# An RWKV-6 block with a two-level expert gate: pairs of heads in a fixed, two-deep engine order, the gate in one pass, whole rows scattered into 224 places per expert

## The chip, the cores and the metric

One Trainium2 chip, one NeuronCore. The metric is the device time of one execution in microseconds (us); three runs of the kernel before gave 718.98, 717.66 and 714.95, median 717.66. Engines are PE (TensorE; PEld is its weight load), DVE (VectorE), ACT (ScalarE), POOL (GpSimd) and SP (SyncE, which issues most DMAs).

## The reference

An RWKV-6 recurrence over 4 batches, 8 heads, 768 steps, head size 48, then a mixture of 16 experts (4 groups of 4) over the 3,072 tokens with 384 channels:

```python
for t in range(S):
    cur = einsum('bhd,bhe->bhde', u * k[t], v[t])
    y[t] = einsum('bhd,bhde->bhe', r[t], state + cur)
    state = w[t][..., None] * state + einsum('bhd,bhe->bhde', k[t], v[t])
x = y as (B*S, H*D)
g = argmax(x @ w_group);  e = argmax(x @ w_expert[g])
out = softmax_g * softmax_e * (relu(x @ w1[g, e]) @ w2[g, e])
```

All of it is float32.

## The kernel before

**First stage, pairs.** Two heads of one batch form a pair; 16 pairs are worked off, each over 6 chunks of 128 steps (12 blocks of 64). `decays` (L240 to L272) runs on DVE and ACT: a reversed scan of the decays (`s`, L248), its reciprocals (L253, L255), a forward scan (`e`, L257), the scaled keys `kk` (L261) and queries `q` (L265), and on ACT `ru` and `tb` (L269, L270). `pair` (L274 to L364) is then a chain through PE: scores of `kk` and `q` and of `k` and `ru` (L282), masked on DVE into `at` (L289, L292); `kk` transposed into `kt` (L299, L301); `kt` times values, the growth of the states (L310), copied by ACT into `g` (L316); a scan on DVE over blocks, `zs` (L320); the inner part, values times `at` (L330); the cross part, `zs` times `q`, into the same banks (L347; half of it waits for a small POOL instruction, `mark`, L338, that follows the inner part); a copy to `xt` (L354), six transposes (L360) and a copy into the token rows `x` (L362). `decays(n+1)` is written ahead of `pair(n)`. All PE results of this stage share one pool of four tiles of two PSUM banks, `banks`.

**Gate.** After four pairs `logits` (L366 on) writes the batch's rows to `x_scratch` in DRAM and makes 24 products with `wr` (20 columns each, L375). `gate` (L381 to L429) runs once a batch, one batch late: it chooses a group, then an expert in it (`choose` twice, L133 to L152), gets each token's rank in its expert by two products with a triangle and with ones (L387, L388) and a loop of 12 small DVE instructions over the chunks, turns the rank into a place, and scatters (token, weight), 8 bytes a token, in six indirect DMAs on POOL's queue (L427). Each of them waits for the one before it, since all write `slot_scratch`.

**Second stage, experts.** Each of 16 experts has 256 static places, two tiles of 128; unused places hold a token number out of bounds. One DMA reads all places (`slots`, L493); two indirect DMAs on POOL fetch an expert's rows from `x_scratch` (L498, 128 rows of 1,536 bytes each); `expert` (L512) transposes them (L519, copy L521), makes the hidden layer in 24 products with 256 columns (L508, relu on ACT L510), the output in 16 products with 384 columns (L527), scales it (L531) and scatters it to `out` (L533). Weights of two experts are held. Beside the first four experts `look` (L538 on) reduces the decays twice a batch (L543, L544) to see whether a slow path is needed. Tokens beyond 256 go through a loop at the end, which runs zero times here.

**What sets the order.** Engines run in order. The program is written pair by pair, but a scheduler that estimates durations reorders each engine's instructions, so that DVE's list mixes pairs, gate and `look`; SP's and POOL's lists are made the same way.

Of the kernel before, what the change touches and what calls it, by code (L numbers as in the profile page):

```python
# [34 lines left out]
C = 64  # L36
JT = 2
CAP = JT * 128
# [5 lines left out]
def rwkv_then_moe(  # L44
# [24 lines left out]
    OV = N - CAP  # L69
    OVT = OV // 128  # L70
    NSTAT = NE * CAP
    NSLOT = NSTAT + NE * OV
    halves = [slice(0, 64), slice(64, 128)]

    x_dram = nc.dram_tensor("x_scratch", (N + 1, DM), F32, kind="Internal").ap()
    slot_dram = nc.dram_tensor("slot_scratch", (NSLOT, 2), F32, kind="Internal").ap()
# [32 lines left out]
    eidx = numbers([128, NE], [[1, NE]], 0, "eidx")  # L109
    thresh = numbers([128, OVT], [[128, OVT]], CAP, "thresh")  # L110
# [8 lines left out]

    seen = const([128, NE], F32, "seen")  # L120
    nc.vector.memset(seen, 0.0)
# [10 lines left out]
    def choose(pool, z, k, n):  # L132


        def small(name, shape):
            return pool.tile([128, n] + shape, F32, name=name, tag=name)

        top, sums = small(f"top{k}", []), small(f"sum{k}", [])
        low, one = small(f"low{k}", [4]), small(f"one{k}", [4])
        nc.vector.tensor_reduce(out=top, in_=z, axis=AX.X, op=ALU.max)  # L140
        tb = top[:, :, None].to_broadcast([128, n, 4])
# [3 lines left out]
        nc.vector.tensor_reduce(out=sums, in_=low, axis=AX.X, op=ALU.add)  # L145
        nc.vector.tensor_scalar(out=sums, in0=sums, scalar1=1e-9, scalar2=None, op0=ALU.add)
        db = desc[:, None, :].to_broadcast([128, n, 4])
        nc.vector.tensor_tensor(out=one, in0=one, in1=db, op=ALU.mult)
        best = small(f"best{k}", [])
        nc.vector.tensor_reduce(out=best, in_=one, axis=AX.X, op=ALU.max)  # L150
        nc.vector.tensor_tensor(out=one, in0=db, op=ALU.is_equal,
                                in1=best[:, :, None].to_broadcast([128, n, 4]))  # L152
        return sums, one

    def experts_of(pool, lg, n, weight):

        gsum, gone = choose(pool, lg[:, :, 0:G], 0, n)
        el = pool.tile([128, n, Eg], F32, name="el", tag="el")
        el4 = pool.tile([128, n, G, Eg], F32, name="el4", tag="el4")
        gob = gone[:, :, :, None].to_broadcast([128, n, G, Eg])  # L160
        nc.vector.tensor_tensor(
            out=el4, in0=lg[:, :, G:].rearrange("p c (g e) -> p c g e", g=G), in1=gob,
            op=ALU.mult)
# [11 lines left out]
    with ExitStack() as first:  # L175
# [6 lines left out]
        def banks():  # L182
            return pp.tile([128, 1024], F32, name="banks", tag="banks")
# [90 lines left out]
        def pair(p, v, xt, x):  # L274
# [28 lines left out]
            def value(c, t, m):  # L303
                o = (c * H + 2 * hp + t) * D
                return v[:, o:o + m]
# [426 lines left out]
```

## Time and profile before

| | us |
|---|---|
| median of 3 runs | 717.66 |
| the profiled execution: its time / its span | 719.73 / 718.0 |
| busy: PE, PEld, DVE, ACT, POOL | 549.1, 439.0, 237.4, 131.8, 106.9 |
| mean granted PE clock | 0.845 of 2.4 GHz |
| from span start to the first score product | 22.3 |
| pairs and gates, to the last logits | 22.3 to 290.9 |
| last gate and hand-over to the experts | 290.9 to 338.4 |
| 16 experts | 338.4 to 702.6 |
| end (last scatter, counters, end of program) | 702.6 to 718.0 |

The shares of busy time are an average over stages with different limits, so each stage is read by itself: in a view of stretches for the busy time of each engine and PE's granted clock (1.00 is 2.4 GHz, 0.50 is 1.2 GHz), and in the timeline for what ended each wait.

### The profile page before, as it was taken

To read this page: it belongs to the slowest core of one execution; us is meant where nothing else is said; L and a number is where in the kernel's file an instruction comes from. 1 tells how busy PE (TensorE), PEld (TensorE's weight loads), DVE (VectorE), ACT (ScalarE), POOL (GpSimd) and SP (SyncE) were. 2 spreads that over 40 slices of the span, in tenths; PEclk is the share of its full clock that TensorE was granted. 3 is DMA by queue.
4 is the path that set the end of the run, shared out by engine and by line. 5 is a ranking of instruction groups with operands and counts; after the bars stand their busy time and mean duration, and the time that the engine had idled before them with its cause. 6 is when DMAs were issued, how large, how long until landed. Compare 5 with 4: busy or idle time off the path is not lost. (4 is left out here: it accounts for less than half of the span.)

```text
span 718.0 us, 12586 instructions
## 1 busy us (share of the span) xinstructions
PE 549.1 (76%) x5490; PEld 439.0 (61%) x5490; DVE 237.4 (33%) x449; ACT 131.8 (18%) x249; POOL 106.9 (15%) x133
## 2 busy tenths in 40 slices
PE   0476886687768688201999999999999999999991
PEld 0466775586658677200776677766777667776670
DVE  3977476638864441664311100111001110011100
ACT  0343233304331321000110111100111001110110
POOL 8000000300030021014022201221112211121100
PEclk9986668756776765555899999999999999999996
DMA  9726358126313004234335445354454635445000
GB/s 218 153 61 164 100 189 275 46 76 155 81 35 100 3 2 134 49 85 113 110 130 214 152 162 192 139 214 138 173 178 153 213 124 191 162 164 193 11 9 20
DMA packets 19777, 91.19 MB, mean 127 GB/s; under 512 B 4585, under 2 KB 7706, under 8 KB 15106
## 3 DMA queue, kind: packets, MB, share of 16 engines
q1 hardware_dynamic: 14850, 79.26, 35.9%
q0 software_dynamic: 4864, 11.04, 4.2%
q8 instruction: 45, 0.74, 0.4%
q14 instruction: 18, 0.15, 0.1%
HBM read 80.43 MB, written 11.43 MB: 128 GB/s over the span
## 5 line engine op out<-in xcount | busy, mean ns | idle before, releaser
L508 PE MATMUL bank_a<-xt,w 128*128 128x256 f32 x768 | 172.3, 385 | 15.4 <-DVE xt L521 15.4
L508 PEld LDWEIGHTS bank_a<-xt,w 128*128 128x128 f32 x768 | 146.2, 192 | 39.0 <-DVE xt L521 19.3
L527 PE MATMUL bank_b<-w,ht 128*128 128x384 f32 x512 | 167.7, 486 | 0.0
L527 PEld LDWEIGHTS bank_b<-w,ht 128*128 128x128 f32 x512 | 97.3, 190 | 64.4
L531 DVE TENSOR_SCALAR yo<-bank_b,slots 128x384 f32<-128x384 f32 x32 | 19.8, 618 | 322.1 <-PE bank_b L527 322.1
L510 ACT ACTIVATE ht<-bank_a 128x256 f32<-128x256 f32 x128 | 49.2, 384 | 349.8 <-PE bank_a L508 349.8
L533 POOL DMA_INDIRECT out_dram<-yo,slots x32 | 32.4, 1014 | 251.6 <-DVE yo L531 243.5
L347 PE MATMUL banks<-q,zs 64*48 64x64 f32 x704 | 41.9, 296 | 36.2 <-DVE zs L320 27.9
L347 PEld LDWEIGHTS banks<-q,zs 64*48 64x48 f32 x704 | 38.3, 198 | 38.9 <-DVE zs L320 30.1
L427 POOL DMA_INDIRECT slot_scratch<-pack,dest x24 | 27.1, 1130 | 110.7 <-DVE dest L425 70.9
L282 PE MATMUL banks<-q,kk 64*64 64x64 f32 x768 | 25.0, 316 | 22.3 <-DVE q L265 22.3
L519 PE MATMUL bank_b<-ident,xg 128*128 128x128 f32 x96 | 13.8, 282 | 36.2 <-DMA xg<-x_scratch,slots 36.2
L375 PEld LDWEIGHTS banks<-wr,xt 128*128 128x128 f32 x192 | 41.5, 333 | 0.0
L375 PE MATMUL banks<-wr,xt 128*128 128x20 f32 x192 | 41.1, 378 | 0.0
L498 POOL DMA_INDIRECT xg<-x_scratch,slots x32 | 30.9, 966 | 61.3 <-PE bank_b L519 52.1
L282 PEld LDWEIGHTS banks<-q,kk 64*64 64x64 f32 x768 | 22.0, 220 | 25.9 <-DVE q L265 22.3
L519 PEld LDWEIGHTS bank_b<-ident,xg 128*128 128x128 f32 x96 | 11.9, 146 | 41.2 <-issue 39.2
L360 PE MATMUL banks<-ident,xt 128*128 128x128 f32 x96 | 24.7, 429 | 14.5 <-ACT xt L354 14.5
L248 DVE TENSOR_TENSOR_SCAN s<-w,first_of 128x780 f32<-128x780 f32 x16 | 28.4, 1773 | 14.8 <-DMA w<-in_w_dram 11.0
L360 PEld LDWEIGHTS banks<-ident,xt 128*128 128x128 f32 x96 | 18.3, 221 | 17.8 <-ACT xt L354 17.8
L257 DVE TENSOR_TENSOR_SCAN e<-w,iv 128x780 f32<-128x780 f32 x16 | 28.5, 1781 | 0.5
L310 PE MATMUL banks<-v,kt 64*64 64x48 f32 x704 | 15.7, 232 | 16.6 <-ACT kt L301 16.6
(120 smaller groups left out, 413.6 us busy)
## 6 DMA issues: line engine op xcount, KB each, us to landing
w<-in_w_dram SPq DMA_DIRECT2D x32, 1536.0 KB, 6.7
rk<-in_rk_dram SPq DMA_DIRECT2D x32, 288.0 KB, 5.0
w<-in_w_dram SPq DMA_DIRECT2D x32, 146.2 KB, 6.2
wt<-in_w_dram SPq DMA_DIRECT2D x4, 1170.0 KB, 7.5
v<-in_v_dram SPq DMA_DIRECT2D x4, 1152.0 KB, 7.4
x_scratch<-x SPq DMA_DIRECT2D x4, 1152.0 KB, 4.8
xg<-x_scratch,slots POOLq DMA_INDIRECT x32, 5.1
out_dram<-yo,slots POOLq DMA_INDIRECT x32, 3.5
```

What stands on the lines that cost most here:

```text
L248: nc.vector.tensor_tensor_scan(out=s[:, 0:WP][:, ::-1], data0=w[:, ::-1], data1=first_of[:, ::-1], initial=1.0, op0=ALU.mult, op1=ALU.add)
L257: nc.vector.tensor_tensor_scan(out=e, data0=w, data1=iv, initial=0.0, op0=ALU.mult, op1=ALU.add)
L282: nc.tensor.matmul(z[halves[j], 512 * t + C * c:512 * t + C * (c + 1)], lhsT=lhs[hs, sl], rhs=rhs[hs, sl], start=True, stop=True)
L347: m = nc.tensor.matmul(y[j][64 * t:64 * t + D, C * c:C * (c + 1)], lhsT=zs[halves[t], :, i], rhs=q[halves[t], C * i:C * (i + 1)], start=Fa ...
L360: nc.tensor.transpose(z[:, c * 128:(c + 1) * 128], xt[:, c * 128:(c + 1) * 128], ident)
L375: nc.tensor.matmul(lv[:, c], lhsT=xts[hp][:, c * 128:(c + 1) * 128], rhs=wr[:, hp], start=(hp == 0), stop=(hp == HP - 1))
L427: nc.gpsimd.indirect_dma_start(out=slot_dram, out_offset=bass.IndirectOffsetOnAxis(ap=dest[:, c:c + 1], axis=0), in_=pack[:, c, :], in_off ...
L498: nc.gpsimd.indirect_dma_start(out=xg, out_offset=None, in_=x_dram, in_offset=bass.IndirectOffsetOnAxis(ap=slot[:, 0:1].bitcast(I32), axis=0))
L508: nc.tensor.matmul(z[:, 0:128 * nt], lhsT=w1[:, dc, f * 128:(f + 1) * 128], rhs=xt[:, dc], start=(dc == 0), stop=(dc == DC - 1))
L510: nc.scalar.activation(out=ht[:, f], in_=z[:, 0:128 * nt], func=AF.Relu)
L527: nc.tensor.matmul(z[:, 0:DM], lhsT=ht[:, f, j * 128:(j + 1) * 128], rhs=w2[:, f], start=(f == 0), stop=(f == FC - 1))
L533: nc.gpsimd.indirect_dma_start(out=out, out_offset=bass.IndirectOffsetOnAxis(ap=slot[:, 0:1].bitcast(I32), axis=0), in_=yo, in_offset=None ...
```

## The change

- **Order.** The pair is cut into pieces, and a loop of 17 rounds writes them out with a fixed order for PE, DVE and ACT. Round n holds the pieces of pair n up to the inner part, the cross part, rows and logits of pair n-1, and the decays of pair n+1. PSUM is split: two score tiles (two banks each), one tile `y` (two banks), two single banks for all else.
- **Logits** are made in two goes: 18 products when three pairs of a batch are done, six after the fourth.
- **Gate.** `choose` runs once on all five groups of four logits (the group's and four experts'); ranks come from a scan over chunks, so the two PE products have 16 columns and the loop over chunks goes.
- **Rows.** `x` is 386 wide (row, token number, weight) and is scattered whole (1,544 bytes a token) into `slot_scratch`, six indirect DMAs with no waits between them; `x_scratch` isn't written on the main path. An expert has 224 places (tiles of 128 and 96), read by two plain DMAs on SP's queue; no gather is left on POOL. Unused places must be filled first: `blanks` writes 16 times 224 rows (346 KB each), four a round in rounds 0 to 3.
- **Experts.** Hidden products have 224 columns.

```diff
-JT = 2
-CAP = JT * 128
+TILES = (128, 96)
+CAP = sum(TILES)
...
-        pp = first.enter_context(tc.tile_pool(name="psum_t", bufs=4, space=PSUM))
+        p_sc = first.enter_context(tc.tile_pool(name="psum_s", bufs=2, space=PSUM))
+        p_y = first.enter_context(tc.tile_pool(name="psum_y", bufs=1, space=PSUM))
+        p_t = first.enter_context(tc.tile_pool(name="psum_t", bufs=2, space=PSUM))
...
+        def blanks(e):
+            nc.sync.dma_start(
+                out=slot_dram[e * NR:e * NR + CAP, :].rearrange("(p j) w -> p (j w)", j=2),
+                in_=blank.rearrange("p j w -> p (j w)"))
...
+        def gate(b, lg, x):
+            mine, gone, low, sums = choose(gp, lg, NCH)
...
+            nc.vector.tensor_tensor_scan(
+                out=upto.rearrange("p e c -> p (e c)"),
+                data0=within.rearrange("p e c -> p (e c)"),
+                data1=mine.rearrange("p e c -> p (e c)"), initial=0.0, op0=ALU.mult, op1=ALU.add)
+            nc.tensor.matmul(cps[:, 0:NE], lhsT=ut, rhs=upto[:, :, NCH - 1], start=True, stop=True)
+            nc.tensor.matmul(cps[:, NE:2 * NE], lhsT=ones, rhs=upto[:, :, NCH - 1], start=True,
+                             stop=True)
...
             for c in range(NCH):
-                nc.gpsimd.indirect_dma_start(
+                put = nc.gpsimd.indirect_dma_start(
                     out=slot_dram,
                     out_offset=bass.IndirectOffsetOnAxis(ap=dest[:, c:c + 1], axis=0),
-                    in_=pack[:, c, :], in_offset=None)
+                    in_=x[:, c, :], in_offset=None)
+                tc.declare_no_dep(put.ins, group="rows", reason="no two tokens have one slot")
...
+        with tc.manual_schedule(engines={ENG.PE, ENG.DVE, ENG.Activation}):
+            for n in range(TOTAL + 1):
+                if n < TOTAL:
+                    p = pipe[n]
...
+                    if n + 1 < TOTAL:
+                        z = pipe[n + 1] = suffixes(n + 1)
+                    masked(p)
+                    if z:
+                        products(z)
+                    keys(p)
+                if n:
+                    outer(pipe[n - 1])
+                if n < TOTAL:
+                    growth(p)
+                    if z:
+                        scaled(z)
+                        prefixes(z)
+                    states(p)
+                    if z:
+                        queries(z)
+                    inner(p)
...
+                    for e in range(4 * n, min(4 * n + 4, NE)):
+                        blanks(e)
...
+                if n:
+                    finish(n - 1)
+                    if ready and (n % HP == 2 or n == TOTAL):
+                        gate(*ready.pop(0))
...
+        for m in TILES:
+            xg = row_tile()
+            nc.sync.dma_start(out=xg[0:m], in_=slot_dram[at:at + m, :])
...
-                nc.tensor.matmul(z[:, 0:128 * nt], lhsT=w1[:, dc, f * 128:(f + 1) * 128],
+                nc.tensor.matmul(z[:, 0:n], lhsT=w1[:, dc, f * 128:(f + 1) * 128],
```

(`suffixes` is the scan `s`, `masked` the scores and the mask, `products` is `kk`, `keys` is `kt`, `outer` the cross part and the copy to `xt`, `growth` and `states` the way to `zs`, `scaled` is `ru` and `tb`, `prefixes` the reciprocals and `e`, `queries` is `q`, `finish` the rows and logits.)

PE, one pair in the middle of a batch. Before (L282 scores, L299 and L360 transposes, L310 growth, L330 inner, L347 cross part):

```order
L282 MATMUL banks<-q,kk 64x64 x24
L282 MATMUL banks<-ru,rk_122 64x64 x24
L299 MATMUL banks<-ident,kk 128x128 x6
L310 MATMUL banks<-v_139,kt 64x48 x22
L330 MATMUL banks<-at,v_139 64x64 x24
L347 MATMUL banks<-q,zs 48x64 x22
L360 MATMUL banks<-ident,xt 128x128 x6
```

One round of the change (L304 scores, L322 transposes, L374 cross part, L335 growth, L355 inner; L398 are the logits at a batch's end):

```order
L304 MATMUL scores<-q,kk 64x64 x24
L304 MATMUL scores<-ru,rk_138 64x64 x24
L322 MATMUL bank<-ident,kk 128x128 x6
L374 MATMUL y<-q,zs 48x64 x22
L335 MATMUL bank<-v_156,kt 64x48 x22
L355 MATMUL y<-at,v_156 64x64 x24
L322 MATMUL bank<-ident,xt 128x128 x6
L398 MATMUL bank<-wr,xt 128x20 x18
```

The seven pieces are the same; the cross part and the second transposes now belong to the pair before and stand where PE had waited for `kt`, `zs` and `xt` of its own pair.

DVE, one round of the change (L258 is `s` and L266, L280, L282, L284, L289 the rest of the next pair's decays; L311, L314 the mask; L345 `zs`):

```order
L258 SCALAR_TENSOR_TENSOR s_178<-w_143,first_of 128x780
L311 TENSOR_TENSOR at<-scores,later 128x768
L314 COPY_PREDICATED at<-diag_mask,scores 128x768
L266 TENSOR_TENSOR kk<-rk_140,s_178 128x768
L280 TENSOR_SCALAR iv_180<-s_178 128x12
L282 RECIPROCAL iv_180<-iv_180 128x12
L284 SCALAR_TENSOR_TENSOR e<-w_143,iv_180 128x780
L345 SCALAR_TENSOR_TENSOR zs<-g_185,tb_183 128x576
L289 TENSOR_TENSOR q<-rk_140,e 128x768
```

Nine instructions a pair as before, now always in this order; the next round's scores wait for the last of them, `q`.

DVE in the last gate of the change, from its first selection to the ranks (L604, L605 are the two reductions of `look`; L408 the scan over chunks):

```order
L159 TENSOR_TENSOR ones_3168<-ones_3168,desc 128x120
L604 TENSOR_REDUCE ends<-wt 96x1
L160 TENSOR_REDUCE best<-ones_3168 128x30
L605 TENSOR_REDUCE ends<-wt 96x1
L161 TENSOR_TENSOR ones_3168<-desc,best 128x120
L166 TENSOR_TENSOR mine<-ones_3168 128x6x16
L408 SCALAR_TENSOR_TENSOR upto_c<-within,mine 128x96
```

Two of `look`'s reductions still stand inside the last gate, ahead of its ranks; before, three of them stood ahead of the places.

## Rows read from the trace of the kernel before

**Rows 1.** Groups of the page: busy, mean ns; idle before, what ended it

```profile
L282 PE MATMUL banks<-q,kk 64*64 64x64 f32 x768 | 25.0, 316 | 22.3 <-DVE q L265 22.3
```

**Rows 2.** Stretches: length, busy by engine (instructions), PE clock, DMA share, GB/s

```profile
core 0: us, PE busy (x) PEld busy (x) DVE busy (x) ACT busy (x) POOL busy (x), PEclk, DMA share, GB/s
280.40:290.90 10.50, 10.47 (x50) 10.35 (x49) 0.00 (x0) 0.64 (x1) 0.00 (x0) 0.50 0.47 148
290.90:338.40 47.50, 1.14 (x4) 0.93 (x4) 29.79 (x64) 0.45 (x2) 9.57 (x10) 0.50 0.38 91
338.40:702.60 364.20, 348.76 (x1378) 255.79 (x1378) 41.05 (x68) 49.17 (x128) 58.53 (x59) 0.99 0.42 150
```

**Rows 3.** Timeline of one pair: start, duration, engine, line, idle before and releaser

```profile
40.00 1.56 PE L282 MATMUL banks<-q,kk 64*64 64x64 f32 x48
41.33 1.50 PE L282 MATMUL banks<-ru,rk 64*64 64x64 f32 x48
...
42.70 0.23 DVE L255 RECIPROCAL iv<-iv 128x12 f32<-128x12 f32 x1
42.77 1.54 PE L299 MATMUL banks<-ident,kk 128*128 128x128 f32 x6
...
42.93 1.01 DVE L292 COPY_PREDICATED at<-diag_mask,banks 128x768 f32<-128x768 uint8 x1
43.84 1.76 DVE L257 TENSOR_TENSOR_SCAN e<-w,iv 128x780 f32<-128x780 f32 x1
...
45.20 0.84 PE L310 MATMUL banks<-v,kt 64*64 64x48 f32 x42 [0.89 <-ACT kt L301]
...
45.93 0.88 PE L330 MATMUL banks<-at,v 64*64 64x64 f32 x46
...
46.91 1.36 DVE L320 TENSOR_TENSOR_SCAN zs<-g,tb 128x576 f32<-128x576 f32 x1 [0.45 <-ACT g L316]
...
48.18 1.76 DVE L248 TENSOR_TENSOR_SCAN s<-w,first_of 128x780 f32<-128x780 f32 x1
...
48.32 2.60 PE L347 MATMUL banks<-q,zs 64*48 64x64 f32 x44 [1.51 <-DVE zs L320]
...
51.83 1.54 PE L360 MATMUL banks<-ident,xt 128*128 128x128 f32 x6 [0.91 <-ACT xt L354]
52.16 0.93 DVE L265 TENSOR_TENSOR q<-rk,e 128x768 f32<-128x768 f32 x1
```

**Rows 4.** Timeline of PE and DVE in the last gate

```profile
293.47 3.34 DVE L543 TENSOR_REDUCE ends<-wt 96x1 f32<-96x3072 f32 x1
...
301.56 0.64 PE L388 MATMUL banks<-one,ones 128*128 128x96 f32 x2
...
304.39 0.25 DVE L395 TENSOR_TENSOR before<-banks,before 128x96 f32<-128x96 f32 x1
```

**Rows 5.** Timeline of POOL: a scatter in the pairs, one in the tail, a gather

```profile
139.50 2.51 POOL L427 DMA_INDIRECT slot_scratch<-pack,dest  x1 [4.36 <-DMA slot_scratch<-pack,dest]
...
311.87 0.96 POOL L427 DMA_INDIRECT slot_scratch<-pack,dest  x1 [37.25 <-DVE dest L425]
...
333.53 0.96 POOL L498 DMA_INDIRECT xg<-x_scratch,slots  x1 [0.31 <-issue]
```

**Rows 6.** DMA issues: queue, count, KB each, median us from issue to landing

```profile
x_scratch<-x SPq DMA_DIRECT2D x4, 1152.0 KB, 4.8
xg<-x_scratch,slots POOLq DMA_INDIRECT x32, 5.1
out_dram<-yo,slots POOLq DMA_INDIRECT x32, 3.5
slot_scratch<-empty SPq DMA_DIRECT2D x1, 384.0 KB, 8.8
```

**Rows 7.** Timeline of PE in the second expert

```profile
365.42 10.63 PE L508 MATMUL bank_a<-xt,w 128*128 128x256 f32 x48 [0.98 <-DVE xt L521]
375.88 10.48 PE L527 MATMUL bank_b<-w,ht 128*128 128x384 f32 x32
```

More of the change, by code (lines that the diff above doesn't have):

```diff
@@ L337, in pair, with inner @@
-            mark = p2.tile([1, 1], F32, name="mark", tag="mark")
-            behind = nc.gpsimd.memset(mark, 0.0)
-            for m in inner:
-                tc.add_manual_dep(behind.ins, m.ins.name, AFTER, reason="row tiles share a bank")
+        def inner(p):
+            z = p["z"] = p_y.tile([128, 1024], F32, name="y", tag="y")
+            p["y"] = [z[:, 512 * j:512 * j + S // 2] for j in range(2)]
+            mark = p2.tile([1, 1], F32, name="mark", tag="mark")
+            ms = [nc.tensor.matmul(p["y"][j][halves[t], C * c:C * (c + 1)],
+                                   lhsT=value(p, c, t, 64)[halves[j]],
+                                   rhs=p["at"][halves[j], t, c], start=(c == 0), stop=False,
+                                   skip_group_check=True)
+                  for c, j, sl in blocks for t in range(2)]
+            p["behind"] = nc.gpsimd.memset(mark, 0.0)
+            for m in ms:
+                tc.add_manual_dep(p["behind"].ins, m.ins.name, AFTER,
+                                  reason="row tiles share a bank")
@@ L341, in pair, with outer @@
+        def outer(p):
             for cross in range(2):
@@ new lines, in gate, with batch, finish @@
+                tc.declare_no_dep(put.ins, group="rows", reason="no two tokens have one slot")
+                tc.add_to_no_dep_group("rows", put.ins)
+        def batch(n):
+            return n // HP
+        TOTAL = B * HP
+        pipe, xs, part, ready = {}, {}, {}, []
+        def finish(n):
+            b, hp = batch(n), n % HP
+            p = pipe.pop(n)
+            rows(p, xs[b])
+            xts[hp] = p["xt"]
+            if hp == HP - 2:
+                z = logits([(h, xts[h]) for h in range(HP - 1)])
+                part[b] = small("part", [NL])
+                nc.scalar.copy(out=part[b], in_=z)
+            if hp == HP - 1:
+                z = logits([(hp, xts[hp])])
+                lg = small("lg", [NL])
+                nc.vector.tensor_tensor(out=lg, in0=z, in1=part[b], op=ALU.add)
+                ready.append((b, lg, xs[b]))
@@ L642, in rwkv_then_moe @@
     nc.vector.memset(ends, 1.0)
-    xgs = {0: [gather(slots[:, 0, j]) for j in range(JT)]}
+    tiles = {0: list(tiles_for(0))}
     for e in range(NE):
         if e + 1 < NE:
-            xgs[e + 1] = [gather(slots[:, e + 1, j]) for j in range(JT)]
-        expert(xgs.pop(e), lambda j: slots[:, e, j], *weights.pop(e))
+            tiles[e + 1] = list(tiles_for(e + 1))
+        expert(tiles.pop(e), *weights.pop(e))
+        if e == 1:
+            where, count_i = overflow()
         if e + 2 < NE:
```

505 lines of the change are left out of this document (242 added, 263 removed).

## The prediction

> **What bounds the kernel now.** I read the stretches first, then the timeline in each of them, then the DMA table. The reader should see three stages with three limits. In the experts, the stretch from 338.40 [rows 2], PE is busy 348.8 of 364.2 us at a granted clock of 0.99: only less PE work helps there. In the hand-over, from 290.90 [rows 2], PE does 1.1 us of work in 47.5: it is a chain of DVE, POOL and DMA steps. In the pairs, from the first score product at 22.3 [rows 1] to 290.9, a stretch of 268.6 us, no engine is full. A pair takes PE 1.56 + 1.50 + 1.54 + 0.84 + 0.88 + 2.60 + 1.54 = 10.5 us, and then PE waits for `kt` 0.89, for `zs` 1.51 and for `xt` 0.91 [rows 3], so that the pair that begins at 40.0 gives way to the next at 53.3. DVE's nine instructions a pair are 1.76 (`s`) + 1.76 (`e`) + 1.36 (`zs`) + 1.01 (mask) + 3 times 0.93 (`q`, and `kk` and the first mask, of the same shape) + 2 times 0.23 = 9.1 [rows 3].
>
> **Pairs.** The change puts work of two other pairs into PE's three waits, and removes none of the seven pieces. A round is then as long as the longer of two sums. DVE's is 9.1, or 9.6 with an estimated 0.05 between instructions: `q` is last in a round and the next scores wait for it, while DVE goes on with `s` of the pair after. PE's depends on the clock. In [rows 3] five of the seven pieces run at the lower level (1.2 GHz) and growth and inner at the upper one: 0.84 and 0.88 for about as many instructions as the scores do in 1.56. All at the lower level gives 11.8 (growth and inner at about 1.55), all at the upper one about 5.9, below DVE. So a round lies between 9.6 and 11.8. I take 10.7, PE's sum as measured, 10.5, and a hand-over of 0.2, since that row has the nearest mix. ACT has fewer us than either and hides; so do the two-bank PSUM tiles, whose copies ACT makes while PE is in the next piece.
>
> The logits stay at 24 products a batch, 10.3 us, and the stretch that holds them, from 280.40 [rows 2], shows PE full at a clock of 0.50, so nothing of them gets cheaper. Split 18 and 6, they are 7.7 and 2.6. What hides is PE's idle time at the end of a round, between nothing and 9.6 - 5.9 = 3.7; the short distance between 10.7 and 9.6 says little hides. I take 7.0 four times and 2.0 three times (the last six fall into the hand-over's head, below).
>
> The gate costs PE a wait, since its two products stand in PE's fixed order: about eight DVE instructions of 0.25 [rows 4], 2.2 with hand-overs, and two products of 0.6 [rows 4], 3.4 in all if the rest of the gate finds DVE idle; if DVE is the bound, all its 19 instructions count, 5.0. I take 4.2, three times. What queues behind it is the next round's scores, and behind DVE's part the next `s`.
>
> Sum: first round 9.6, 15 rounds at 10.7 = 160.5, logits 28 + 6, gates 12.6: 216.7. Then the last pair's cross part 2.6, copy to `xt` 0.9, transposes 1.5, a bank to come free 0.5, six logits 2.6: 8.1. Together 224.8 against 268.6: **43.8 us less**. Bounds: all at DVE's pace 16 times 9.6, logits 4 times 4.0, gates 3 times 5.0, plus 8.1 = 192.7 (76 less); all at the lower clock 9.6 + 15 times 11.8 + 4 times 7.7 + 3 times 2.6 + 3 times 3.4 + 8.1 = 243.5 (25 less).
>
> What is added beside this: scatters of 1,544 bytes a token take POOL about as long as the old ones. Six in a row delay the next `mark`, which half of the cross part waits for; six times 1.27 (0.96 and 0.31 of gap, [rows 5]) is 7.6, and the cross part comes more than a round later, so it costs nothing. `blanks` adds 5.5 MB of writes in rounds 0 to 3, 1.4 MB a round. At the rate of the row of 1,152 KB in 4.8 us [rows 6] that is 5.8 us a round, and a round's own loads (868 KB) 3.6: 9.4 within 10.7, with each load asked for two rounds ahead. Hidden, barely. Loading and the first decays, to 22.3, stay.
>
> **Hand-over.** From the last logits: addition and first selection on DVE 1.2, two reductions of `look` still inside, 2 times 3.34 [rows 4], selection and scan 1.2, the two products 1.2, ranks and places 1.7, gaps 0.2: places at 12.2. Six scatters one behind the other: the last begins at 12.2 + 0.3 + 5 times 1.27 = 18.8, lands 3.5 later (the row of `out`, of the same size, [rows 6]), at 22.3. SP's load of the first rows: issue 0.4, landing between 3.5 and the gather's 5.1 [rows 6]; I take 4. Transposes at 26.7 against 47.5: **20.8 us less**. Gone are the six landings in series, the read of all places and the gather behind it. Bounds: if each scatter takes the 2.51 of one row in the pairs [rows 5], 7.7 more, 13 less in all; if the load lands in 2 us, 23 less.
>
> There a rule of the Trainium skill speaks against the change. The trace first: most scatters take 0.96, and one in the pairs took 2.51 [rows 5]. The page "SBUF — State Buffer", section "Who interferes with whom", says that VectorE instructions with two SBUF inputs contend with GpSimd instructions that read SBUF. By that rule the six scatters, which now go out while DVE works off the counting of overflows, would stretch, and the sum would be up to 7.7 us higher than by the 0.96 row. The tail's row with 0.96 went out beside such instructions too, so I stay with the row.
>
> **Experts.** 48 instructions with 256 columns take 10.63, 32 with 384 take 10.48 [rows 7]: 221 and 327 ns, 0.83 ns a column and 9 ns fixed. With 224 columns that is 195 ns, 9.36 us: 1.27 less. Three transposes and one copy to `xt` (PE waits 0.98 for it [rows 7]) shrink by a quarter, 0.1 an expert, perhaps 0.15. The output products stream 384 columns as before, whatever the tile's height. 16 times 1.4 = **22.4 us less** (20.3 to 24). Loads by SP in place of gathers by POOL stand three experts ahead and hide; if they came late, PE would wait for the first transposes of an expert. End and overflow loop: as before; the largest expert of these inputs has 220 tokens by the reference, under 224.
>
> **Total.** 43.8 + 20.8 + 22.4 = 87.0. The profiled execution took 719.73 (span 718.0): 632.7. The median of the runs is 2.1 below that execution: **631**.
>
> **Rivals.**
> 1. *DVE sets the pace.* PE without waits keeps the upper clock, a round is 9.6. For it: [rows 3] show the clock up after a run of pieces without a gap. Against it: then PE idles 3 us a round, and the 1.51 before the cross part, in the same rows, was followed by pieces at the lower level. Rounds 16 times 9.6, logits 20 and 1.5, gates 15, 8.1: 198 us, 27 less than forecast, so 604.
> 2. *The lower clock throughout.* For it: the logits ran full at 0.50, so being busy alone does not raise the clock. 243.5 in the pairs: 649.
> 3. *Scatters stretch* (the mechanism of the 2.51 row): 7.7 in the tail, and in the pairs six times 2.8 = 17 us on POOL, which makes `mark` some 2 us late in three rounds: 644.
> 4. *Blanks flood the queue: slower than before.* The old filling of 384 KB landed only after 8.8 us [rows 6]. If each blank took that rate, 7.9, a round 0 to 3 would take four of them and 3.6 of loads, 35.3 in place of 10.7: 98 more, 729. It is slower than before from (87 / 4 + 10.7 - 3.6) / 4 = 7.2 us a blank. Against it: that row was issued while the first loads filled the queue, and x_scratch got three times as much written in 4.8.
> 5. *The 224 don't hold* (the change not doing what it says): each tile that overflows pays exposed weights (two loads) and half an expert, about 25: 656 with one.
>
> **How the numbers follow.** Forecast 0.43; rivals 0.20, 0.20, 0.10, 0.05, 0.02. The range leaves out rival 4 and the outer half of the bounds: 604 to 659 are the ends of rivals 1 and of all lower terms together, so 604 to 658. Faster by over 0.5% (about what a measurement of this kernel can tell from no change, 3.6 us) 0.92; within it 0.03, for a flood that just eats the gain; slower 0.05.
>
> **What would show it.** Right: score products of neighbouring pairs 10 to 11.5 apart without logits, no wait of PE for `kt` or `zs`, a clock between 0.6 and 0.9 there; last logits near 247; 25 to 28 us from there to the first expert's transposes, six scatters 1.3 apart; experts 21.2 apart. Wrong: PE waiting for DVE's `q` each round (rival 1); seven pieces at 11.8 (rival 2); scatters over 2 us (rival 3); DVE's `s` or `kk` waiting for DMA in rounds 1 to 5 (rival 4); a second set of weight loads at the end (rival 5).

## The result, and the profile after

The change takes 619.65 us (median of four runs, 617.93 to 620.49) against 716.31 for the kernel before, measured beside it: a ratio of 0.8644, 95% interval 0.8607 to 0.8681. The forecast was 631, range 604 to 658. In a later set of runs the same kernel took 605.39, a ratio of 0.8435 (0.8366 to 0.8504); what that difference of 14 us consists of is shown in experiment 5. The profiled execution took 620.24, its span is 618.4.

Stretches of the change: length, busy by engine (instructions), PE clock, DMA share, GB/s. They stand beside [rows 2]:

```profile
core 0: us, PE busy (x) PEld busy (x) DVE busy (x) ACT busy (x) POOL busy (x), PEclk, DMA share, GB/s
22.60:239.60 217.00, 175.76 (x4108) 160.16 (x4108) 147.70 (x199) 78.17 (x149) 22.42 (x34) 0.85 0.49 144
239.60:264.20 24.60, 1.02 (x5) 0.97 (x5) 21.98 (x37) 0.30 (x1) 6.12 (x6) 0.50 0.40 113
264.20:606.10 341.90, 326.99 (x1378) 248.02 (x1378) 46.77 (x73) 45.70 (x128) 29.64 (x31) 0.99 0.48 165
606.10:618.40 12.30, 0.09 (x1) 0.00 (x1) 0.68 (x2) 0.00 (x0) 0.92 (x1) 0.61 0.06 18
```

Against the kernel before, the pairs lost 51.6 us (268.6 to 217.0), the hand-over 22.9 (47.5 to 24.6), the experts 22.3 (364.2 to 341.9), the end 3.1 (15.4 to 12.3). The head is as it was: first score product at 22.60 against 22.3 [rows 1].

A round without logits or gate, from the timeline of PE and DVE, which answers to [rows 3]:

```profile
80.30 1.16 PE L304 MATMUL scores<-q,kk 64*64 64x64 f32 x48
...
80.61 1.77 DVE L258 TENSOR_TENSOR_SCAN s<-w,first_of 128x780 f32<-128x780 f32 x1
81.28 0.88 PE L304 MATMUL scores<-ru,rk 64*64 64x64 f32 x48
82.09 0.87 PE L322 MATMUL bank<-ident,kk 128*128 128x128 f32 x6
82.89 2.35 PE L374 MATMUL y<-q,zs 64*48 64x64 f32 x42
...
85.09 0.94 PE L335 MATMUL bank<-v,kt 64*64 64x48 f32 x41
...
85.57 1.78 DVE L284 TENSOR_TENSOR_SCAN e<-w,iv 128x780 f32<-128x780 f32 x1
86.25 0.93 PE L355 MATMUL y<-at,v 64*64 64x64 f32 x48 [0.22 <-ACT xt L382]
...
87.27 1.33 DVE L345 TENSOR_TENSOR_SCAN zs<-g,tb 128x576 f32<-128x576 f32 x1
88.52 0.93 DVE L289 TENSOR_TENSOR q<-rk,e 128x768 f32<-128x768 f32 x1
...
89.51 0.79 PE L304 MATMUL scores<-q,kk 64*64 64x64 f32 x35 [1.53 <-DVE q L289]
```

PE's waits for `kt` and `zs` are gone, and 0.22 is left of the one for `xt`. One wait of 1.53 for `q` stands in their place. The granted clock is 1.00 over the whole round of 9.2, and PE is busy 7.46 of it. The cross part takes 2.35 even there.

The hand-over, from the timeline; it answers to [rows 4 to 6]:

```profile
239.58 0.28 DVE L455 TENSOR_TENSOR lg<-bank,part 128x120 f32<-128x120 f32 x1 [13.52 <-PE bank L398]
...
240.92 3.34 DVE L604 TENSOR_REDUCE ends<-wt 96x1 f32<-96x3072 f32 x1
...
244.37 3.34 DVE L605 TENSOR_REDUCE ends<-wt 96x1 f32<-96x3072 f32 x1
...
251.05 0.32 DVE L426 TENSOR_REDUCE dest<-upto_c 128x6 int32<-128x96 f32 x1
252.12 1.32 POOL L429 DMA_INDIRECT slot_scratch<-x,dest  x1 [26.43 <-DVE upto L524]
...
258.80 0.96 POOL L429 DMA_INDIRECT slot_scratch<-x,dest  x1 [0.30 <-issue]
...
261.47 2.70 SPq L558 DMA_DIRECT2D xg<-slot_scratch  x6
...
264.18 1.35 PE L579 MATMUL bank_b<-ident,xg 128*128 128x128 f32 x6 [14.38 <-DMA xg<-slot_scratch]
```

The reader sees the chain as it was summed: two reductions inside the gate, places 11.8 after the start of the addition, then six scatters, the first 1.32 long and the rest 0.96 with 0.30 between them, the load, the transposes.

An expert, from PE's timeline, beside [rows 7]; the period is 309.09 - 287.88 = 21.2:

```profile
287.88 0.74 PE L579 MATMUL bank_b<-ident,xg 128*128 128x128 f32 x6
...
289.58 9.35 PE L567 MATMUL bank_a<-xt,w 128*128 128x224 f32 x48 [0.96 <-DVE xt L581]
298.77 10.48 PE L589 MATMUL bank_b<-w,ht 128*128 128x384 f32 x32
309.09 0.74 PE L579 MATMUL bank_b<-ident,xg 128*128 128x128 f32 x6
```

### The profile page after: what moved, and what is told of

It reads as the page before. It is cut to its first block, busy times and chain, and to the rows that moved or that the text cites. A ratio compares the mean times of both kernels' runs of the same rounds, so it can differ in the third digit from the quotient of the medians.

```text
span 618.4 us, 12610 instructions
## 1 busy us (share of the span) xinstructions
PE 503.9 (81%) x5490; PEld 409.2 (66%) x5490; DVE 228.6 (37%) x344; ACT 127.5 (21%) x281; POOL 74.3 (12%) x103
## 5 line engine op out<-in xcount | busy, mean ns | idle before, releaser
L589 PE MATMUL bank_b<-w,ht 128*96 128x384 f32 (+1 forms) x512 | 167.7, 486 | 0.0
L567 PE MATMUL bank_a<-xt,w 128*128 128x224 f32 x768 | 151.9, 358 | 14.9 <-DVE xt L581 14.9
L589 PEld LDWEIGHTS bank_b<-w,ht 128*96 128x96 f32 (+1 forms) x512 | 90.4, 176 | 70.1 <-issue 38.3
L593 DVE TENSOR_SCALAR yo<-bank_b,xg 128x384 f32<-128x384 f32 (+1 forms) x32 | 19.7, 616 | 287.9 <-PE bank_b L589 287.9
L569 ACT ACTIVATE ht<-bank_a 128x224 f32<-128x224 f32 x128 | 45.7, 357 | 309.6 <-PE bank_a L567 309.6
L595 POOL DMA_INDIRECT out_dram<-yo,xg x32 | 30.6, 955 | 317.6 <-DVE yo L593 274.4
L304 PE MATMUL scores<-q,kk 64*64 64x64 f32 x768 | 21.0, 270 | 34.8 <-DVE q L289 31.2
L304 PEld LDWEIGHTS scores<-q,kk 64*64 64x64 f32 x768 | 17.9, 177 | 37.0 <-DVE q L289 32.6
L374 PEld LDWEIGHTS y<-q,zs 64*48 64x48 f32 x704 | 37.1, 199 | 3.5 <-issue 3.5
L374 PE MATMUL y<-q,zs 64*48 64x64 f32 x704 | 39.4, 268 | 0.0
L398 PE MATMUL bank<-wr,xt 128*128 128x20 f32 x192 | 32.7, 325 | 5.2 <-ACT x L390 5.2
L398 PEld LDWEIGHTS bank<-wr,xt 128*128 128x128 f32 x192 | 31.8, 262 | 7.1 <-ACT x L390 7.1
L429 POOL DMA_INDIRECT slot_scratch<-x,dest x24 | 27.1, 1130 | 54.8 <-DVE upto L524 26.4
L258 DVE TENSOR_TENSOR_SCAN s<-w,first_of 128x780 f32<-128x780 f32 x16 | 28.4, 1775 | 9.8 <-DMA w<-in_w_dram 9.8
L345 DVE TENSOR_TENSOR_SCAN zs<-g,tb 128x576 f32<-128x576 f32 x16 | 21.6, 1353 | 21.2 <-ACT g L340 20.0
L284 DVE TENSOR_TENSOR_SCAN e<-w,iv 128x780 f32<-128x780 f32 x16 | 28.5, 1783 | 0.6
L335 PE MATMUL bank<-v,kt 64*64 64x48 f32 x704 | 20.1, 230 | 5.7 <-issue 5.4
L579 PEld LDWEIGHTS bank_b<-ident,xg 128*128 128x128 f32 (+1 forms) x96 | 11.5, 146 | 19.6 <-issue 19.6
L579 PE MATMUL bank_b<-ident,xg 128*128 128x128 f32 (+1 forms) x96 | 12.5, 268 | 14.4 <-DMA xg<-slot_scratch 14.4
L311 DVE TENSOR_TENSOR at<-scores,later 128x768 f32<-128x768 f32 x16 | 15.1, 944 | 24.4 <-PE scores L304 24.4
```

The lines of the kernel that those rows point to most:

```text
L258: nc.vector.tensor_tensor_scan(out=s[:, 0:WP][:, ::-1], data0=w[:, ::-1], data1=first_of[:, ::-1], initial=1.0, op0=ALU.mult, op1=ALU.add)
L284: nc.vector.tensor_tensor_scan(out=p["e"], data0=p["w"], data1=p["iv"], initial=0.0, op0=ALU.mult, op1=ALU.add)
L304: nc.tensor.matmul(z[halves[j], 512 * t + C * c:512 * t + C * (c + 1)], lhsT=lhs[hs, sl], rhs=rhs[hs, sl], start=True, stop=True)
L345: nc.vector.tensor_tensor_scan(out=p["zs"].rearrange("p e c -> p (e c)"), data0=p["g"].rearrange("p e c -> p (e c)"), data1=p["tb"].rearra ...
L374: m = nc.tensor.matmul(p["y"][j][64 * t:64 * t + D, C * c:C * (c + 1)], lhsT=p["zs"][halves[t], :, i], rhs=p["q"][halves[t], C * i:C * (i ...
L398: nc.tensor.matmul(z[:, c], lhsT=xt[:, c * 128:(c + 1) * 128], rhs=wr[:, hp], start=(hp == hps[0][0]), stop=(hp == hps[-1][0]))
```

## The experiments

Beside the edit shown, all kernels here differ from the change in one added copy in the slow path that never runs. The first four kernels ran on one chip, the next four on a second, the next three on a third, the last on a fourth; the chip of the change's first runs is not known. So stages are compared before totals, and totals across chips with care.

**1. One pair in flight.** The pair's end goes back into its own round.

```diff
-                if n:
-                    outer(pipe[n - 1])
...
-                if n:
-                    finish(n - 1)
-                    if ready and (n % HP == 2 or n == TOTAL):
-                        gate(*ready.pop(0))
+                if n < TOTAL:
+                    outer(p)
+                    finish(n)
+                if ready and (n % HP == 1 or n == TOTAL):
+                    gate(*ready.pop(0))
```

> The cross part, the rows and the logits of a pair go back into the pair's own round; everything else stays as in the change (fixed order, split logits, new gate, whole rows, 224 places). Theory (the pairs got shorter because work of another pair fills PE's three waits): a plain round goes from 9.2 to 10.3 back to about the 13.3 of the kernel before, 15 times about 3 to 3.7, so the pairs get 45 to 56 us longer and the whole takes 665 to 676; the waits of PE for kt, zs and xt are back, about 0.9, 1.5 and 0.9 a pair. Rival (the fixed order, the split logits and the new gate made the gain, the second pair in flight little): 0 to 15 us longer, 620 to 635, with rounds under 11.

Measured: 671.05, ratio 0.9344 (0.9316 to 0.9372). Plain rounds are 13.2 to 13.4, as in the kernel before (13.3). The stretches of its pairs and its hand-over, and a round's waits in PE's timeline:

```profile
22.50:290.20 267.70, 211.84 (x4108) 189.92 (x4108) 147.12 (x198) 81.12 (x149) 28.92 (x34) 0.65 0.40 117
290.20:314.70 24.50, 1.05 (x5) 1.00 (x6) 22.74 (x40) 0.30 (x1) 6.14 (x6) 0.50 0.41 114
```

```profile
102.37 1.18 PE L335 MATMUL bank<-v,kt 64*64 64x48 f32 x44 [0.30 <-ACT kt L329]
...
106.83 2.58 PE L374 MATMUL y<-q,zs 64*48 64x64 f32 x44 [2.57 <-DVE zs L345]
...
110.32 1.54 PE L322 MATMUL bank<-ident,xt 128*128 128x128 f32 x6 [0.91 <-ACT xt L382]
```

The pairs are back at 267.7, against 268.6 before the change: without the second pair in flight the whole gain of that stage is gone. It comes twice: the waits are filled, and the same 4,108 instructions keep PE busy 175.8 in place of 211.8, at a clock of 0.85 in place of 0.65. With one pair in flight the new gate, the split logits and the fixed order bring next to nothing there (0.9); what they are worth beside two was not measured.

**2. `kk` made twice on DVE, and `kk` made on POOL.**

```diff
+            again = p2.tile([128, S], F32, name="again", tag="again", bufs=1)
+            nc.vector.tensor_tensor(
+                out=blocked(again), in0=blocked(p["rk"][:, 1]), op=ALU.mult,
...
```

(`xt` is also held in four buffers in place of five.)

> DVE makes the product kk twice in every round (the second result is thrown away), 0.93 to 0.98 us more on DVE and nothing on the other engines. Theory (in rounds without logits DVE sets the pace, PE waits for q): the six or seven rounds in which PE waits for q get 0.9 to 1.0 longer each, the head 1.0, gate rounds some 0.5: 7 to 10 us longer in all, 627 to 630, with plain rounds at 10.2 to 11. Rival (PE and its clock set the pace): only the head's 1.0 and perhaps 1 to 2 more, 620 to 622, with plain rounds as before and less wait for q.

```diff
-            nc.vector.tensor_tensor(
+            nc.gpsimd.tensor_tensor(
                 out=blocked(kk), in0=blocked(p["rk"][:, 1]), op=ALU.mult,
```

> The product kk is made by POOL in place of DVE; nothing else changes. If DVE sets the pace and POOL's instruction does not slow DVE's down: plain rounds fall by up to 0.9, to 8.4 to 9.3, gate rounds by about as much, 5 to 9 us less in all, 611 to 615. If POOL's instruction (two SBUF inputs) stretches DVE's instructions beside it, as scatters were stretched beside DVE's scans, or takes so long itself that the next scores wait for kk: 0 to 15 us longer, 620 to 635. If PE sets the pace: within 1 us of the change.

Measured: 630.01 (ratio 0.8788, 0.8747 to 0.8830) and 625.50 (0.8709, 0.8676 to 0.8742). With `kk` twice the plain rounds 0, 5, 9 and 13, 9.2 to 9.3 in the change, are 10.0 to 10.4, and the head is 1.2 longer; rounds 1 and 2 don't get longer. Round 0 is the clean sign: it is 9.1 to 9.3 in every kernel with two pairs in flight that leaves DVE's row alone, while round 5 varies there from 9.2 to 11.0 and round 13 from 9.2 to 10.2 without any such edit. So DVE's sum does set the shortest rounds. The total agrees with the expectation partly by chance: the pairs got 8 us longer, of which the plain rounds give 2.9; rounds 7, 11 and 15, where scatters go out, give 6.4, and the others are 1.0 shorter.

With 0.94 taken off DVE round 0 falls to 8.6, rounds 1 and 2 to 9.7 and 9.4, but rounds 5, 9 and 13 rise to 10.2 to 10.5. POOL's instruction does not stretch DVE's in these rounds: it takes 1.69 and begins when `s` has ended, and the mask product beside it stays at 0.93. Round 13 of the kernel with `kk` on POOL:

```profile
196.23 1.52 PE L304 MATMUL scores<-ru,rk 64*64 64x64 f32 x48
...
197.30 0.93 DVE L311 TENSOR_TENSOR at<-scores,later 128x768 f32<-128x768 f32 x1
197.46 1.69 POOL L266 TENSOR_TENSOR kk<-rk,s 128x768 f32<-128x768 f32 x1 [5.27 <-DVE s L258]
197.68 1.54 PE L322 MATMUL bank<-ident,kk 128*128 128x128 f32 x6
...
202.40 0.74 ACT L340 COPY g<-bank 128x288 f32<-128x288 f32 x2
...
203.17 1.36 DVE L345 TENSOR_TENSOR_SCAN zs<-g,tb 128x576 f32<-128x576 f32 x1 [1.68 <-ACT g L340]
...
204.45 0.93 DVE L289 TENSOR_TENSOR q<-rk,e 128x768 f32<-128x768 f32 x1
```

DVE now waits 1.68 for ACT's `g`, and `q` stands behind `zs`. Two limits lie at about one height: DVE's nine instructions, and the chain scores, `kt`, growth, `g`, `zs`, `q` through three engines, whose length moves with PE's clock (scores and transposes 1.5 each here, 0.87 in the change's rounds). That neither theory had. Why the clock is at the lower level at the start of this round is not shown.

In the head a scan does meet POOL's product, and there it is stretched, to 2.89 against 1.78 in the change; the head is 2.25 longer:

```profile
20.34 1.68 POOL L266 TENSOR_TENSOR kk<-rk,s 128x768 f32<-128x768 f32 x1 [4.29 <-DVE s L258]
...
20.76 2.89 DVE L284 TENSOR_TENSOR_SCAN e<-w,iv 128x780 f32<-128x780 f32 x1
```

**3. Scatters of 8 bytes a token.** The rows are not scattered, and the experts work on unused places, so only the pairs are compared.

```diff
-                    out=slot_dram,
+                    out=thin_dram,
...
-                    in_=x[:, c, :], in_offset=None)
+                    in_=x[:, c, DM:], in_offset=None)
```

> Left out: the rows themselves are not scattered, only 8 bytes a token (token number and weight) go to a table of their own, with the same places, the same six instructions and descriptors of 128 rows; the experts then work on unused places and write nothing. So only the stretch of the pairs is compared, not the whole. In the change, the rounds 7, 11 and 15, where six scatters go out beside 18 logits, take 21.3, 17.9 and 19.7 against 16.1 of round 3, where no scatters go out, with short idle times on PE that nothing in the profile releases. If the bytes of the rows on the DMA engines or at the SBUF cause these, the three rounds fall to 16 to 17, the pairs by 8 to 11 us. If POOL's work on the scatters (instructions and descriptors) causes them, the rounds stay at 18 to 21. If it is something else in those rounds (clock, order), they stay too, and no scatter is at work in the idle times.

One execution: rounds 7 and 11 take 21.6 and 21.6. The bytes of the rows are not the cause. What the idle times look like, in the change's own round 7 (PE and POOL; `issue` stands for idle time that nothing in the profile ends):

```profile
112.22 1.81 POOL L429 DMA_INDIRECT slot_scratch<-x,dest  x1 [0.30 <-issue]
...
112.96 0.68 PE L335 MATMUL bank<-v,kt 64*64 64x48 f32 x28 [0.39 <-issue]
...
115.61 0.33 PE L355 MATMUL y<-at,v 64*64 64x64 f32 x3 [0.37 <-issue]
...
118.82 7.87 PE L398 MATMUL bank<-wr,xt 128*128 128x20 f32 x36
```

Growth and inner part come in pieces, the inner part of three to six instructions every 0.7 us, and the 18 logits behind them run at a granted clock of 0.50 (7.87).

**4. The gate one round later; the reductions later; 256 places; scatters that wait.**

```diff
-                    if ready and (n % HP == 2 or n == TOTAL):
+                    if ready and (n % HP == 3 or n == TOTAL):
```

> The gates of the first three batches stand one round later, behind the 18 logits of the round, so that DVE makes the selection while PE works on the logits, and the six scatters go out beside the round after it (which has six logits) and no longer beside the round with 18. Two questions. First, PE's wait for DVE's selection (4.1 and 4.3 us seen ahead of the gate's first product, three gates): if it hides behind the logits, rounds with a gate cost 2 to 4 us less each, 6 to 12 in all. Second, the short idle times of PE in the rounds with 18 logits and scatters (round 3 without scatters 16.1; rounds 7, 11, 15: 21.3, 17.9, 19.7): if the scatters cause them, the rounds with 18 logits all fall to about 16 plus the gate's two products, and the rounds behind them, with six logits and scatters, rise from 11.9 by 2 to 5, no gain; if it is the scatters together with the many logits (the clock falls after the idle times, and the 18 logits then run at the lower level), the gain is 6 to 10. Together: 607 to 616 in the first case, 600 to 609 in the second; 618 to 622 if neither holds.

Measured: 606.43, ratio 0.8431 (0.8408 to 0.8453), just under the first case's range. Rounds 6, 10 and 14, which had the gate, fall from 15.8, 12.2, 13.2 to 13.3, 8.8, 8.8; rounds 8 and 12, which now have the scatters, rise from 11.9 and 11.8 to 17.1 and 16.6; rounds 7 and 11 are 19.9 and 13.6. PE's wait for the selection in these three gates, 11.6 in the change, is gone: the selection hides behind the logits, and the idle times go where the scatters go. The profiled execution took 611.54, and its pairs are 208.1, 8.9 less than the change's.

```diff
-        if e < B:
-            look(e)
+        if 4 <= e < 4 + B:
+            look(e - 4)
```

> The reductions of the decays for the slow path move from the first four experts to the experts from the fifth on, behind data that only arrives there, so that none of them stands inside the last gate. Theory (two reductions of 3.34 each lie on the chain from the last logits to the places, nothing else covers them): the hand-over falls from 24.6 by 6.7 to 17.9, and 612 to 614 in all; the experts that get them lose at most 1 or 2, if a copy to xt waits behind a reduction. Rival (something else ends last there, a load of weights or of values): under 3 us less, 617 to 621.

(The columns of `ends` are also set from rows of the fifth expert, so that the reductions cannot be put earlier.) Measured: 622.90, ratio 0.8677 (0.8632 to 0.8721). The hand-over is 18.3 (245.86 to 264.19), 6.3 less, as by the theory; but the fourth expert takes 24.7 in place of 21.2, since two reductions (at 324.78 and 328.57) stand ahead of the outputs of the expert before it and of its own copy to `xt`, and the pairs, left alone by the edit, were 222.8. The total does not show the gain, the stage does.

```diff
-TILES = (128, 96)
+TILES = (128, 128)
```

> 256 places per expert in place of 224 (two tiles of 128); nothing else. By the terms of the sum the experts take 1.4 us more each, 16 times, 22.4 in all; blanks of 395 KB in place of 338 stay hidden: 641 to 643. The end, from the last scaled output to the end of the program, took 12.3 against 15.4 of the kernel before: if the height of the last tile (96 rows against 128) makes the difference, it goes back to about 15 and the whole to 644 to 646; if not, it stays at 12 to 12.6. If the blanks are at the edge of what the rounds hide, rounds 0 to 4 get longer, by up to 1.4 each, 5 in all.

Measured: 647.52, ratio 0.9011 (0.8978 to 0.9043). An expert takes 22.59 against 21.20 (transposes at 317.31 and 339.90): 1.39, the term was 1.4. The total is 4.5 above the expectation's upper end, and the pairs, left alone but for larger blanks, are 221.3 against 217.0. The end is 12.5, so the last tile's height is not what shortened it.

```diff
-                tc.declare_no_dep(put.ins, group="rows", reason="no two tokens have one slot")
-                tc.add_to_no_dep_group("rows", put.ins)
```

> The six scatters of a gate wait for one another again, as in the kernel before (they go to one table, and nothing says that no two tokens have one place). Theory: in the hand-over five landings come into the chain, by the rows of before 15.4 us from the first to the last scatter against 6.4, 9 more; in the pairs the series takes 15 to 27 us on POOL, and the small instruction that half of the cross part waits for stands behind it, so that PE waits in the round after, 5 to 10 us three times: 634 to 660 in all, PE's wait being named as that instruction. Rival (the landings are covered by the counting and by loads, and the pairs have room for POOL's series): under 5 us more, 619 to 625.

Measured: 621.98, ratio 0.8643 (0.8608 to 0.8679), as fast as the change, and for neither reason. The profiled execution, the slowest of four, took 628.09. Its stretches:

```profile
22.70:232.20 209.50, 171.88 (x4108) 157.67 (x4108) 147.52 (x198) 77.95 (x149) 21.59 (x33) 0.82 0.51 147
232.20:271.60 39.40, 1.01 (x5) 0.96 (x5) 26.18 (x41) 0.30 (x1) 7.20 (x7) 0.50 0.40 111
```

The hand-over is 14.8 longer (forecast 9), so the missing waits are worth that there. The pairs are 7.5 shorter than in the change's profile: rounds 7 and 11 take 17.1 and 16.9, without the idle times.

**5. The change again, and combinations.**

> The change itself, beside the next two on one chip; it differs in one instruction of the slow path that never runs, which all kernels of these experiments share. 617 to 623. Its rounds with 18 logits and scatters (21.3, 17.9, 19.7 in the one profile so far) took 21 to 23 in four other kernels that leave those rounds alone: here they should lie between 17 and 22 again; if all three lie near 21.5, the profile of the change was a lucky one of a spread, and differences of 3 to 4 us between experiments there mean nothing.

Measured: 605.39, ratio 0.8435 (0.8366 to 0.8504). Its stretches and its round 7:

```profile
22.30:225.40 203.10, 166.61 (x4108) 152.98 (x4108) 147.62 (x198) 77.81 (x149) 26.34 (x34) 0.87 0.54 154
225.40:250.20 24.80, 1.00 (x4) 0.96 (x5) 22.00 (x37) 0.30 (x1) 6.12 (x6) 0.50 0.40 112
```

```profile
111.26 0.94 PE L335 MATMUL bank<-v,kt 64*64 64x48 f32 x41
112.42 0.93 PE L355 MATMUL y<-at,v 64*64 64x64 f32 x48 [0.22 <-ACT xt L382]
...
115.25 6.84 PE L398 MATMUL bank<-wr,xt 128*128 128x20 f32 x36 [1.10 <-ACT x L390]
```

The 13.9 us between the two profiles of the change lie almost wholly in three places: round 7 (21.3, 17.2), round 11 (17.9, 14.3) and from round 15 to the last logits (27.4, 21.3). These are the rounds with scatters, and here the idle times are missing. So my expectation missed, that these rounds would lie between 17 and 22 and the whole between 617 and 623. Of the 13.9, 9.2 are PE's busy time (175.76 against 166.61) and 4.7 its idle time.

```diff
-                tc.declare_no_dep(put.ins, group="rows", reason="no two tokens have one slot")
-                tc.add_to_no_dep_group("rows", put.ins)
+                if b == B - 1:
+                    tc.declare_no_dep(put.ins, group="rows", reason="no two tokens have one slot")
+                    tc.add_to_no_dep_group("rows", put.ins)
```

> The later gate, and the scatters of the first three gates wait for one another again (the last gate's do not). From the two runs before: with waits between scatters the rounds with 18 logits and scatters took 17 in place of 21.5, and with the later gate the scatters stood in rounds 8 and 12 (17.1 and 16.6 against 11.9 of round 4). Theory (six scatters one behind the other leave PE short idle times, whatever bytes they move): these rounds fall to 12 to 13, 8 to 10 less than the later gate alone (606): 595 to 599. Rival (the later gate already took what there was; or POOL's long series makes the small instruction ahead of the cross part late): 603 to 610.

(The gate stands one round later here too, as in experiment 4.) Measured: 620.81, ratio 0.8653 (0.8590 to 0.8715): 15 slower than the change on the same chip. The rival's second reason is what happened, but its price was too low by 11. PE's and POOL's timeline:

```profile
147.79 0.09 POOL L360 MEMSET mark<- 1x1 f32 x1
...
147.94 1.43 PE L374 MATMUL y<-q,zs 64*48 64x64 f32 x21 [11.12 <-POOL mark L360]
```

The scatters that wait hold POOL's queue, the small `mark` stands behind them, and half of the cross part waits 11.12 for it: round 9 takes 23.3. In the tail the third batch's series also runs into the last gate's, and the hand-over is 28.7.

> As the last one, and the reductions for the slow path stand right behind the copies to xt of the experts 4, 6, 8 and 10, one pair of them an expert, where DVE has nothing else to do for some 15 us. The earlier move took 6.3 off the hand-over but put 3.5 into one expert, where two pairs of reductions stood in a row ahead of an output and a copy. Theory: 6 to 6.7 less than the last kernel, with all experts from the second on at 21.2: 588 to 593. Rival (weights or the reductions' own loads come late behind one another on SP's queue): 1 to 5 us of it lost again, 593 to 598.

Its edit is the last one together with the next one's reductions. Measured: 620.26, ratio 0.8598 (0.8528 to 0.8667), over 20 above the expectation. No expert loses (21.2 each from the second on), but PE waits 13.9 for `mark`, and the hand-over is still 25.4, since the last gate's first scatter stands behind the third batch's series.

```diff
-                    if ready and (n % HP == 2 or n == TOTAL):
+                    if ready and (n % HP == 3 or n == TOTAL):
...
+        if beside is not None:
+            look(beside)
         ht = hidden(xt, w1, n)
...
+        b = (e - 4) // 2 if e in range(4, 4 + 2 * B, 2) else None
+        if b is not None:
+            nc.vector.tensor_scalar(out=ends[:, :, b], in0=tiles[e][0][0][:, 0:2],
+                                    scalar1=0.0, scalar2=1.0, op0=ALU.mult, op1=ALU.add)
+        expert(tiles.pop(e), *weights.pop(e), b)
...
-        if e < B:
-            look(e)
```

> The later gate with scatters one behind the other as in the change (no waits between them), and the reductions for the slow path in the experts 4, 6, 8 and 10. From the stages of the runs before: hand-over 18 (the last addition of the logits to the first transposes) in place of 24.6; experts 21.2 each from the second on; no wait of PE for the small POOL instruction (11.1 in the kernel with spaced scatters); pairs as in the later gate alone. 598 to 602, if PE's short idle times beside the scatters are there (rounds 8 and 12 near 17); 588 to 595 if they are missing, as in the second run of the change (rounds 8 and 12 near 12). Rival (the moves only push waits elsewhere): 604 to 610.

Measured: 591.76 (median of six), ratio 0.8255 (0.8225 to 0.8284), the fastest kernel here, 13.6 below the change's better set. Its stretches:

```profile
21.80:216.10 194.30, 161.70 (x4108) 148.15 (x4108) 147.24 (x198) 77.59 (x149) 20.51 (x32) 0.87 0.55 158
216.10:234.50 18.40, 1.01 (x5) 0.94 (x5) 10.02 (x36) 0.30 (x1) 8.06 (x8) 0.50 0.34 118
234.50:576.30 341.80, 326.81 (x1378) 247.86 (x1378) 59.63 (x78) 45.77 (x128) 29.68 (x31) 0.99 0.50 169
```

Against the change's second profile that is 8.8 less in the pairs, 6.4 in the hand-over and nothing in the experts, as expected for the case without idle times beside the scatters (588 to 595). Idle times beside the scatters are missing here too (rounds 8 and 12: 11.7 and 11.5).

## Why the prediction was right

**Pairs**, forecast 43.8 less (224.8 in all), measured 51.6 less (217.0), and 203.1 in the second profile. The mechanism held: experiment 1 gives the whole gain back. Of the signs named in advance, the clock (0.85), the scatters' distance and the experts came out; plain rounds of 10 to 11.5 and last logits near 247 did not (9.2 to 10.3, and 239.5), and rival 1's sign is there, PE's wait of 1.53 for `q`. The sizes, forecast against the two profiles:
- Plain rounds 10.7: mean 9.6 and 9.8 over rounds 1, 2, 5, 9 and 13. I had taken PE's sum at the mixed clock. Without the waits the clock goes up, PE's pieces sum to less than DVE's row, and rival 1's price was the right one for these rounds. Its reason is half right: DVE's row and the chain through `g` end at about the same time (experiment 2). My bound of 5.9 for PE at the upper level was too low (7.46 busy in the round above), since the cross part doesn't halve: 42 instructions take 2.35 at a clock of 1.00, 44 take 2.60 at 0.50.
- Rounds with six logits 12.7: 11.4 to 12.2. "Nothing of them gets cheaper" was wrong: six products take 1.51 at the upper level against 2.75 in the tail at the lower.
- Gate rounds 14.9: mean 13.7 and 13.3; the first of them, 15.8 and 16.0, is longest by a wait of another kind (last section).
- Rounds with 18 logits 17.7: 16.1 and 16.7 without scatters, 21.3, 17.9, 19.7 with them in the first profile, 17.2, 14.3, 13.6 in the second. The sentence on the scatters, "it costs nothing", failed in the first profile, where they cost some 10 us against three times round 3's 16.1; rival 3 had a price there, but for `mark`, which made PE wait in neither profile of the change (with one pair in flight it did, 4.3 in all).
- From the last cross part to the last logits 8.1: 7.8 and 7.7.

**Hand-over**, 20.8 less: 22.9. Places at 11.8 (forecast 12.2), the last scatter 19.2 in (18.8), transposes at 24.6 (26.7): the load was issued 2.7 after that scatter began and landed 2.7 later, where I had 3.5 and 4.4. On the rule of the Trainium skill, page "SBUF — State Buffer", section "Who interferes with whom": in the pairs the scatters at 107.46 and 112.22 take 1.76 and 1.81 against 0.96, and each overlaps one of DVE's scans (from 106.50 to 108.27 and from 111.48 to 113.26), as the rule has it. In the tail only the first stretched, to 1.32: 0.4, not 7.7. But this is a weak test, since DVE's instructions with two inputs overlap only the first, the second and the sixth of them, each 0.54 at most; beside the fourth and the fifth runs a reduction of `look`, which has one input. The row I set against the rule was misread in the same way: the old tail's scatter at 311.87 took 0.96 beside such a reduction (311.51, 3.34), not beside the counting. So the term of the tail came out, but the reason that I gave for it does not hold.

**Experts**, 22.4 less: 22.3, and 1.39 each by experiment 4. **Blanks** stayed hidden: rounds 1 and 2 are at most 1.1 longer than the shortest, and round 2 holds an idle time of another kind of 1.42 (last section); rival 4's 729 is far off. **The end** was forecast as before and lost 3.1, nearly all of it behind the last scatter (13.5 before, 10.5 now); the height of the last tile isn't the reason, and what is stays open.

So the total erred by +11 in the first set (12.5 for the profiled execution, forecast at 632.7), in the plain rounds (5.4), gates (3.5), six logits (2.6), the end (3.1) and the hand-over (2.1), against 4.3 too little for the rounds with scatters; by 26 in the second, where these 4.3 turn into 9 too much and the time, 605.39, is nearly rival 1's 604. That the first set lies as near to 631 as it does is in part luck: idle times beside the scatters, which the sum put at nothing, cover a part of what the plain rounds were given too much.

## What to carry to other kernels

Filling an engine's waits with a neighbour's work can pay twice: here the same products got cheaper, since PE had the upper clock for more of the time; so cost the pieces at the clock that the new order gives, not at that of the old. Once the waits are gone, look for the second limit at the same height before taking work off the first: 0.94 off DVE shortened the first rounds and not the later ones, where a chain through three engines ended at about the same time. Read an edit by its stage and not by the total alone: a 6.3 us gain in the hand-over was lost to sight behind other stages, and one waiting scatter series cost 11 us through a one-element instruction queued behind it.

## What was not expected of the hardware

**PE's idle times beside scatters** that go out one behind another. They stood in all profiles with such scatters in the pairs from the first set and the next two chips (the change, 8-byte rows, `kk` twice and on POOL, the later gate, the later reductions, 256 places; small ones with one pair in flight). They were all but missing in the kernel whose scatters wait, on the same chip as three of these. They are not due to the rows' bytes. But on the last two chips the change and the fastest kernel had scatters just as dense (0.30 apart) and no such idle times, so dense scatters are not enough; the two spaced kernels that ran on one of these chips therefore say nothing. Whether the chip, the placement in memory or something else decides stays open: one kernel was not run on several chips side by side. The pairs of the change's two profiles differ by 13.9 us, more than twice the spread of its runs in either set (2.6 and 6.5), so two sets of runs of one kernel can differ by more than either's interval says.

**Idle times at fixed places of PE's list.** Some longer waits without a releaser stand outside the scatters, in the change for example:

```profile
92.04 0.39 PE L304 MATMUL scores<-q,kk 64*64 64x64 f32 x11 [1.74 <-issue]
```

With 1.42 at 44.19 and 1.41 at 98.06 it lengthens rounds 2 and 6. The second profile has them at the same instructions (0.66, 1.74 and 1.68). Counted over PE's recorded products and weight loads these are the 962nd, the 3,010th and the 3,267th, 2,048 and 257 apart. A queue named `instruction` moved 45 packets of 16 KB in the change, for 10,980 such instructions: one for some 244, if all of them are PE's. So the loading of PE's instructions is the likely reason; no run varied it. With one pair in flight no wait of PE without a releaser is over 0.4 in the pairs. The idle times beside the scatters do not stand at such distances: several of them come within some 140 instructions.
